# Windowed attention before two feed-forward layers on one core: fillers, weight words and first loads at the head

## Chip, cores, metric

One Trainium2 chip, one core of it. The metric is the device time of one execution in microseconds; the time of a kernel is the median over its runs. Before the change three runs gave 887.54 us in the median (884.97 to 889.1).

## What is computed

Two parts in a row, on 2304 tokens of 512 features. First attention: 4 batches, 8 heads of 64, 512 local and 32 global positions each; a local query sees the local keys within 32 positions and all global keys, a global query sees everything. Then two feed-forward layers, 512 to 2048 and back, with different functions in the middle.

```python
s_g = scale * q_g @ k_all.T                       # k_all: global, then local keys
out_g = softmax(s_g) @ v_all
s_ll = where(abs(i - j) <= 32, scale * q_l @ k_l.T, -1e9)
out_l = softmax(concat(scale * q_l @ k_g.T, s_ll)) @ concat(v_g, v_l)
x = concat(out_g, out_l)                          # tokens x 512
h = x @ moe_w_in;  x = (h * sigmoid(h)) @ moe_w_out
h = x @ moe2_w_in; y = (h * cos(h)) @ moe2_w_out
```

The weights are handed over as 64-bit floats; the kernel reads them as pairs of 32-bit words and makes 32-bit floats of them on the chip. Every product of the feed-forward layers is taken as three matmuls of a high and a low part.

## The kernel before

**Units.** The local attention is cut into units: one pair of heads, 256 queries, in four windows of 64. There are 32 units; the first eight, `EARLY`, are unit 0 to unit 7. They make up the inputs of the first feed-forward tile (512 tokens) and are done before it: this is the head. A unit has loads of k, of two halves of q (one a head, `load_qk`, lines 226 and 229) and of v (`load_v`, line 242), all issued from SP; its scores on TensorE (`unit_scores`, line 252); mask and maximum on VectorE (`unit_max`, line 268); the exponential on ScalarE (`unit_exp`, line 278); the normalisation on VectorE (`unit_norm`, lines 286 to 289); copies of the global columns on GpSimd (`unit_glob_parts`, lines 301 and 302); two groups of transposes on TensorE (lines 324 and 310) with their copies on ScalarE (lines 328 and 314); the products with the values on TensorE (`unit_values`, lines 351 and 358); and a high and a low part of the result, on ScalarE and VectorE (`unit_x`, lines 369 and 371).

**Fillers.** `keep_going` (line 337) issues matmuls of zeros into a part of a bank that nobody reads. `begin` does so between the first scores (8, 4, 6, 6 and 6 of 512 columns), and `unit_values` in every unit of the head, `PAUSE` = 6 of 256 columns before the products.

**Weights.** A chunk is one `(f, part)` of the first layer: 128 x 512 floats as pairs of words, 512 KB, loaded by `load_w1` (line 121). `rebias` shifts the high word (line 131) and the low word (line 132) on ScalarE; `to_f32` puts them together on VectorE (lines 138 and 142); `split_w_hi` makes the high part, on GpSimd for the chunks in `POOLED` (line 159) and on ScalarE for the others (line 161); `split_w_lo` the low part on VectorE (line 165). The first five chunks in the order of need are all in `POOLED`.

**Order.** All is planned by hand: `at(rank, step, fn, ...)` puts a function at a step, and `run` issues the steps in order and, within a step, by rank. `plan_early_unit` gives unit n its steps around n - 9: scores three steps earlier, maximum one step earlier, exponential, normalisation and copies at n - 9, transposes a step later, values two steps later. The shifts of chunk i fall on step i - 4, at a rank ahead of the GpSimd copies of a unit; its floats one step and its low part two steps later. Steps -12 to -1 are kept in this order as they stand; steps 0 to 35 may be reordered by the scheduler; from 36 on they are kept again. The first feed-forward tile begins at step 0. Each engine works through its queue in order, and so does SP. Ahead of all steps stand the loads: q and k of units 0, 1 and 2, v of unit 0, the global values, then unit 3, and so on, with the weight chunks from unit 5 on between them; a load waits until the eighth load before it has landed.

Of the kernel before, what the change touches and what calls it, by code (L numbers as in the profile page):

```python
# [11 lines left out]
F32 = mybir.dt.float32  # L12
# [3 lines left out]
AF = mybir.ActivationFunctionType  # L16
ALU = mybir.AluOpType
# [23 lines left out]
REBIAS = 2.0**-112  # L41
# [7 lines left out]
def attention_then_two_ffn(  # L49
# [9 lines left out]
    nc = tc.nc  # L59
# [56 lines left out]
    def slot(part, f, dtype=F32):  # L116
        return wts.tile([128, 1024], dtype, tag=f"w{part}_{f}", name="w")
# [10 lines left out]

    def rebias(ph, f, part):
        low, high = (W[ph, f, part][:, :, i] for i in range(2))  # L130
        nc.scalar.activation(out=high.bitcast(F32), in_=high.bitcast(F32), func=AF.Copy, scale=REBIAS)
        nc.scalar.activation(out=low, in_=low.bitcast(U32), func=AF.Copy, scale=TOP3, bias=TOP3_BIAS)

    def to_f32(ph, f, part):
# [81 lines left out]
    def load_qk(n):  # L216
        if n >= NU:
            return
        if n < EARLY:
            t = slot(1, NF - 1 - n)[:, 0 : UNIT * (64 + KX)]  # L220
        else:
            t = P["qk"].tile([128, UNIT * (64 + KX)], F32, tag="qk", name="qk")
        q = t[:, 0 : UNIT * 64].rearrange("p (c x) -> p c x", c=UNIT)
        k = t[:, UNIT * 64 :].rearrange("p (c x) -> p c x", c=UNIT)
        src = units[n, :, 0 : UNIT * 128].rearrange("p (c x) -> p c x", c=UNIT)
        nc.sync.dma_start(out=t[:, UNIT * 64 :], in_=units[n, :, UNIT * 128 : QKCOLS])
        for h in range(2):
            part = slice(64 * h, 64 * h + 64)
            nc.sync.dma_start(out=q[part], in_=src[part, :, part])
        A.setdefault(n, {}).update(q=q, k=k)  # L230

    def load_v(n):
# [101 lines left out]
    def keep_going(room, times):  # L334
        moving = zeros.unsqueeze(1).to_broadcast([128, room.shape[1] // 64, 64])
        for _ in range(times):
            nc.tensor.matmul(room[0:64], zeros, moving, start=True, stop=True, skip_group_check=True)
# [4 lines left out]
    def unit_values(n):  # L342
        b, p = n // (2 * NP), n % NP
        a = A[n]
        pool, tag = (ps_y, f"y{n % 2}") if n < EARLY else (ps_a, "a")
        bank = pool.tile([128, 512], F32, tag=tag, name="ps_o")
        a["po"] = po = bank[:, 0 : UNIT * 64].rearrange("p (c x) -> p c x", c=UNIT)
        if n < EARLY:
            keep_going(bank[:, UNIT * 64 :], PAUSE)
        for h in range(2):  # L350
            nc.tensor.matmul(
                po, vst[b][:, p, D * h : D * h + 128], a["pgt"][:, 2 * h : 2 * h + 2, :], start=h == 0, stop=False,
                skip_group_check=True,
            )
        for j in range(UNIT):
            for h in range(2):
                rows = slice(64 * h, 64 * h + 64)
                nc.tensor.matmul(  # L358
                    po[rows, j, :], a["v"][:, j, rows],
                    a["pt"][:, 2 * h + j // 2, 64 * (j % 2) : 64 * (j % 2) + 64], start=False, stop=j == UNIT - 1,  # L360
                    skip_group_check=True,
                )
# [410 lines left out]

    P, M, A, G, H, Y, gq, g32, vst, CH = ({} for _ in range(10))
    EARLY = 2 * NP
    PAUSE = 6
    LEAD, SLACK, LOADS, AHEAD, FIRST, CUT = 9, 3, 6, 8, -4, 36
    LAG = 12
    POOLED = (0, 1, 2, 3, 4, 6, 8, 10)
    head, pre, gemm, pe, post = -20, 0, 10, 20, 40  # L780
    seq = [(t, f) for t in range(len(size[0])) for f in range(NF)]
# [15 lines left out]
    def plan_early_unit(n, s):  # L797
        at(head + 9, s - 3, unit_scores, n)
        at(head, s - 1, unit_max, n)
        at(head + 1, s, unit_exp, n)  # L800
        at(head + 8, s, unit_norm, n)
        at(head + 8, s, unit_glob_parts, n)
        at(head + 4, s + 1, unit_local_t, n)
        at(head + 4, s + 1, unit_glob_parts_t, n)
        at(head + 5, s + 1, unit_p, n)
        at(head + 5, s + 1, unit_glob_parts_p, n)
        at(head + 2, s + 2, unit_values, n)
        at(head + 3, s + 2, unit_x, n, 0)
        at(head + 12, s + 2, unit_x, n, 1)
# [5 lines left out]
    def plan_unit(n, s, after):  # L815
        exp, norm, turn, parts, values, x = (s + i for i in after)
        at(pe + 1, s, unit_scores, n)
        at(post, s, unit_max, n)
        at(pre, exp, unit_exp, n)
        at(pre, norm, unit_norm, n)  # L820
        at(pe + 2, turn, unit_local_t, n)
        at(post, turn, unit_p, n)
        if after is NEAR:
            at(pre, norm, unit_glob_parts, n)
            at(gemm + 25, turn, unit_glob_parts_t, n)
            at(post, turn, unit_glob_parts_p, n)
        else:
            at(pre, turn, unit_glob_t, n)
            at(pre, parts, unit_glob_p, n)
        at(pe, values, unit_values, n)  # L830
        at(post, values, unit_x, n, 0)
        at(pre, x, unit_x, n, 1)
        at(post, s, load_qk, n + 2)
        at(post, values, load_v, n + 1)
# [33 lines left out]
    for b, s in ((1, 11), (2, 47), (3, 64)):  # L868
        plan_vg(b, s)

    chunks = sorted(
        (tick[i] if part == 0 else second[i], f, part)
        for i, (t, f) in enumerate(seq) if t == 0 for part in range(2)
    )
    for i, (need, f, part) in enumerate(chunks):
        s = min(need - SLACK, FIRST + i * (tick[NF] - 3 - FIRST) // (len(chunks) - 1))
        if i >= AHEAD:
            at(post, s - LOADS, load_w1, f, part)
        at(head + 6, s, rebias, 0, f, part)
        at(head + 7, s + 1, to_f32, 0, f, part)  # L880
        at(head + 10, s + 1, split_w_hi, 0, f, part)
        at(head + 6.5, s + 2, split_w_lo, 0, f, part)
# [8 lines left out]
    for i, (f, part) in enumerate(order):  # L891
        s = times[i]
        ready = max([times[i - 2] + 1 if i > 1 else 0, s - 2] + [e + 1 for e in ends if e < s])
        at(pre + 1, ready, load_w2_words, f, part)
        at(post - 1, s, rebias, 1, f, part)
        at(pre, s + 1, to_f32, 1, f, part)
        at(post - 1, s + 1, store_w2, f, part)
    for i in range(HALF):
        for row in (1, 0):
            f = i + HALF * row  # L900
# [51 lines left out]
    for q in range(pairs):  # L952
# [17 lines left out]
        for m, (row, c) in enumerate(todo):  # L970
            s_m = s + LAG + m * 7 // len(todo)
            if q == pairs - 2:
# [6 lines left out]
    attention_pools(p1)  # L979
    make_constants()  # L980
    load_qk(0)
    load_qk(1)
    load_qk(2)
    load_v(0)
# [101 lines left out]
```

## Time and profile before

| | |
|---|---|
| median of three runs | 887.54 us (884.97 to 889.1) |
| the profiled execution | 885.68 us |
| its span | 883.9 us |
| TensorE busy | 866.0 us, 98% |
| VectorE busy | 654.0 us, 74% |
| ScalarE busy | 515.8 us, 58% |
| GpSimd busy | 250.8 us, 28% |
| mean granted clock of TensorE | 0.996 |

The profile is of one execution; its span runs from the first to the last instruction of the program, and its own time is some 2 us longer. Engines are called PE (TensorE), PEld (TensorE's weight loads), DVE (VectorE), ACT (ScalarE), POOL (GpSimd) and SP; a q behind the name means the engine's sequencer. A line such as L131 is the line of the kernel. In a timeline, a row has start, duration, engine, line, operation, out<-in, the count of merged instructions, and in brackets the engine's idle time before it with what ended that. Small tiles share names: q, k, v of the first eight units and the weights are all `w`. The clock is given as a share of full speed.

### The profile page before, as it was taken

How to read it: one execution, taken by the hardware profiler on the slowest of the kernel's cores; microseconds unless marked ns; L12 is line 12 of the kernel's file. 1: busy time of each engine (PE TensorE's matmuls, PEld its weight loads, DVE VectorE, ACT ScalarE, POOL GpSimd, SP SyncE). 2: the span in 40 equal slices, each digit the busy share in tenths (PEclk: the TensorE clock that was granted, in tenths of full speed). 3: DMA queues.
4: the chain of work that ended last, by engine and by line, in shares of the span. 5: the costliest groups of instructions: out<-in, count | busy, mean ns of one | idle time of the engine just before them, and what ended most of it. 6: DMA issues, size and time to landing. Idle time of an engine off the chain costs nothing.

```text
span 883.9 us, 16714 instructions
## 1 busy us (share of the span) xinstructions
PE 866.0 (98%) x5854; PEld 759.2 (86%) x5854; DVE 654.0 (74%) x1531; ACT 515.8 (58%) x1171; POOL 250.8 (28%) x455
## 2 busy tenths in 40 slices
PE   8899999999999999999999999999999999999997
PEld 5677778899888999999988888888998889889996
DVE  4799993687979767677477667888887667876674
ACT  4898962566655655565355464565755446554453
POOL 3221110021222212011010044444444444455530
PEclk9999999999999999999999999999999999999999
DMA  8958520466555755444388769887567555576641
GB/s 264 352 177 290 201 66 13 156 205 195 173 169 160 224 170 159 134 130 145 125 289 277 256 184 295 247 225 188 116 168 196 118 119 119 122 202 143 143 108 60
DMA packets 126179, 156.57 MB, mean 177 GB/s; under 512 B 29072, under 2 KB 85904, under 8 KB 126096
## 3 DMA queue, kind: packets, MB, share of 16 engines
q1 hardware_dynamic: 77712, 111.44, 38.5%
q0 software_dynamic: 48384, 44.06, 21.8%
q8 instruction: 47, 0.77, 0.4%
q14 instruction: 36, 0.29, 0.1%
HBM read 123.47 MB, written 31.98 MB: 176 GB/s over the span
## 4 chain that ended last, share of the span: by engine, by line
PE 77%; DVE 7%; ACT 5%; DMA 3%; issue 2%; POOL 0%; SPq 0%; ACTq 0%; DVEq 0%
PE ps_y L760 7%; PE ps_y L761 7%; PE ps_y L759 7%; PE ps_p L688 6%; PE ps_p L689 6%; PE ps_p L690 6%; PE ps_y L524 6%; PE ps_hid L485 5%; PE ps_hid L487 5%; PE ps_hid L486 5%; PE ps_y L526 5%; PE ps_y L525 5%; PE ps_o L358 1%; PE ps_s L252 1%; DMA raw<-in_w_dram 1%
## 5 line engine op out<-in xcount | busy, mean ns | idle before, releaser
L627 POOL DMA_DIRECT2D w<-w1c x336 | 177.6, 535 | 255.4 <-PE ps_p L690 183.8
L524 PE MATMUL ps_y<-act,w 128*128 128x256 f32 (+2 forms) x384 | 131.8, 343 | 0.0
L485 PE MATMUL ps_hid<-xh,w 128*128 128x256 f32 (+2 forms) x384 | 126.5, 329 | 0.0
L526 PE MATMUL ps_y<-act,w 128*128 128x256 f32 (+2 forms) x384 | 126.1, 328 | 0.0
L525 PE MATMUL ps_y<-act,w 128*128 128x256 f32 (+2 forms) x384 | 126.0, 328 | 0.0
L486 PE MATMUL ps_hid<-xh,w 128*128 128x256 f32 (+2 forms) x384 | 125.8, 328 | 0.0
L487 PE MATMUL ps_hid<-xl,w 128*128 128x256 f32 (+2 forms) x384 | 125.7, 327 | 0.0
L760 PE MATMUL ps_y<-w,g 128*128 128x512 f32 x272 | 107.7, 396 | 0.0
L761 PE MATMUL ps_y<-w,g 128*128 128x512 f32 x272 | 107.4, 395 | 0.0
L759 PE MATMUL ps_y<-w,g 128*128 128x512 f32 x272 | 106.5, 392 | 0.6 <-DVE g L749 0.6
L688 PE MATMUL ps_p<-w 128*128 128x384 f32 (+1 forms) x320 | 105.1, 328 | 1.9 <-ACT area L701 1.8
L689 PE MATMUL ps_p<-w 128*128 128x384 f32 (+1 forms) x320 | 105.5, 330 | 0.0
L690 PE MATMUL ps_p<-w 128*128 128x384 f32 (+1 forms) x320 | 105.1, 329 | 0.0
L720 ACT ACTIVATE area<-area 128x768 int32<-128x768 f32 (+1 forms) x48 | 38.9, 811 | 103.0 <-DVE area L707 65.3
L497 DVE SCALAR_TENSOR_TENSOR act<-act,ps_hid 128x256 f32<-128x256 f32 (+2 forms) x96 | 50.6, 527 | 64.3 <-ACT act L496 64.1
L496 ACT ACTIVATE act<-ps_hid 128x256 f32<-128x256 f32 (+2 forms) x96 | 44.8, 467 | 88.8 <-PE ps_hid L487 88.7
L524 PEld LDWEIGHTS ps_y<-act,w 128*128 128x128 f32 x384 | 72.7, 189 | 10.8 <-issue 4.0
L485 PEld LDWEIGHTS ps_hid<-xh,w 128*128 128x128 f32 x384 | 73.0, 190 | 5.6 <-issue 0.4
L487 PEld LDWEIGHTS ps_hid<-xl,w 128*128 128x128 f32 x384 | 72.9, 190 | 5.2
L486 PEld LDWEIGHTS ps_hid<-xh,w 128*128 128x128 f32 x384 | 73.1, 190 | 4.9
L526 PEld LDWEIGHTS ps_y<-act,w 128*128 128x128 f32 x384 | 72.6, 189 | 5.1
L525 PEld LDWEIGHTS ps_y<-act,w 128*128 128x128 f32 x384 | 72.8, 189 | 4.5
(152 smaller groups left out, 1835.1 us busy)
## 6 DMA issues: line engine op xcount, KB each, us to landing
w<-w1c POOLq DMA_DIRECT2D x336, 128.0 KB, 2.4
w<-in_w_dram SPq DMA_DIRECT2D x32, 512.0 KB, 7.3
raw<-in_w_dram SPq DMA_DIRECT2D x64, 256.0 KB, 3.1
w1c<-w SPq DMA_DIRECT2D x44, 256.0 KB, 3.3
w2f<-w SPq DMA_DIRECT2D x64, 128.0 KB, 3.0
qk<-in_units_dram SPq DMA_DIRECT2D x24, 320.0 KB, 4.2
v<-in_units_dram SPq DMA_DIRECT2D x24, 256.0 KB, 3.2
w<-w2f SPq DMA_DIRECT2D x24, 256.0 KB, 5.1
```

The source lines that it names most:

```text
L485: nc.tensor.matmul(h, lo[:, ws], xh[:, k, :], start=k == 0, stop=False)
L486: nc.tensor.matmul(h, hi[:, ws], xh[:, k, :], start=False, stop=False)
L487: nc.tensor.matmul(h, hi[:, ws], xl[:, k, :], start=False, stop=k == NP - 1)
L524: nc.tensor.matmul(o, lo[:, ds_], gh, start=f == 0 and d % per == 0, stop=False, skip_group_check=True)
L525: nc.tensor.matmul(o, hi[:, ds_], gh, start=False, stop=False, skip_group_check=True)
L526: nc.tensor.matmul(o, hi[:, ds_], gl, start=False, stop=f == NF - 1, skip_group_check=True)
L627: nc.gpsimd.dma_start(out=part, in_=w1c[q % HALF][j][:, i * 256 : i * 256 + 256])
L688: nc.tensor.matmul(bank, lo, xh, start=whole and k == 0, stop=False, skip_group_check=True)
L689: nc.tensor.matmul(bank, hi, xh, start=False, stop=False, skip_group_check=True)
L759: nc.tensor.matmul(y, gl, hi, start=begin_, stop=False)
L760: nc.tensor.matmul(y, gh, hi, start=False, stop=False)
L761: nc.tensor.matmul(y, gh, lo, start=False, stop=end)
```

## The change

Three edits, all of them at the head. The fillers in the values of units 1 to 4 go, those of units 0, 5, 6 and 7 stay. The high words of the first five weight chunks are shifted by GpSimd instead of ScalarE; the low words stay with ScalarE. The q halves of units 0, 1 and 2 are issued from ScalarE's queue instead of SP's.

```diff
     def rebias(ph, f, part):
         low, high = (W[ph, f, part][:, :, i] for i in range(2))
-        nc.scalar.activation(out=high.bitcast(F32), in_=high.bitcast(F32), func=AF.Copy, scale=REBIAS)
+        if ph == 0 and (f, part) in [x[1:] for x in chunks[:BESIDE]]:
+            nc.gpsimd.tensor_scalar(
+                out=high.bitcast(F32), in0=high.bitcast(F32), scalar1=REBIAS, scalar2=1.0, op0=ALU.mult, op1=ALU.mult
+            )
+        else:
+            nc.scalar.activation(out=high.bitcast(F32), in_=high.bitcast(F32), func=AF.Copy, scale=REBIAS)
         nc.scalar.activation(out=low, in_=low.bitcast(U32), func=AF.Copy, scale=TOP3, bias=TOP3_BIAS)
...
         for h in range(2):
             part = slice(64 * h, 64 * h + 64)
-            nc.sync.dma_start(out=q[part], in_=src[part, :, part])
+            (nc.scalar if n < 3 else nc.sync).dma_start(out=q[part], in_=src[part, :, part])
...
-        if n < EARLY:
+        if n in LOOSE:
             keep_going(bank[:, UNIT * 64 :], PAUSE)
...
-    PAUSE = 6
+    PAUSE, LOOSE = 6, (0, 5, 6, 7)
...
-    LAG = 12
+    LAG, BESIDE = 12, 5
```

## Rows read from the trace of the kernel before

**Rows 1.** The page, section 1: busy time, share of the span, instructions:

```profile
PE 866.0 (98%) x5854; PEld 759.2 (86%) x5854; DVE 654.0 (74%) x1531; ACT 515.8 (58%) x1171; POOL 250.8 (28%) x455
```

**Rows 2.** The chain that ended last, in order of time: start, duration, what:

```profile
42.26 1.09 PE ps_tg L310 x4
...
55.43 0.69 DVE w L165
...
111.46 0.47 PE ps_o L351 x2
```

**Rows 3.** Windows: length, busy us of PE, PEld, DVE, ACT, POOL, clock, DMA, GB/s:

```profile
35.00:40.00 5.00, 3.00 (x33) 2.35 (x33) 3.47 (x11) 5.00 (x16) 1.56 (x4) 1.00 1.06 399
...
50.00:110.00 60.00, 58.69 (x378) 46.02 (x376) 57.94 (x129) 55.95 (x120) 9.50 (x15) 1.00 0.74 246
```

**Rows 4.** DMA view of 0:3 (40 slices, queue), 3:8, 8:13 with its q loads:

```profile
DMA  0000000000000000000000095868925529998999
...
q1 hardware_dynamic: 151, 0.31, 35.8%
...
q1 hardware_dynamic: 1709, 1.02, 73.5%
...
q1 hardware_dynamic: 1384, 1.42, 100.7%
...
w<-in_units_dram SPq DMA_DIRECT2D x4, 64.0 KB, 4.5
```

**Rows 5.** Timeline of SP, the q loads of units 0 and 3:

```profile
1.19 1.40 SPq L229 DMA_DIRECT2D w<-in_units_dram  x2
...
8.13 1.27 SPq L229 DMA_DIRECT2D w<-in_units_dram  x2
```

**Rows 6.** Timeline of ScalarE, its first exponential:

```profile
6.48 0.43 ACT L278 ACTIVATE w<-w,st 128x160 f32<-128x160 f32 x1 [4.46 <-DVE st L268]
```

**Rows 7.** Timeline of TensorE, the scores of units 3 and 7:

```profile
13.10 0.97 PE L252 MATMUL ps_s<-w 64*64 64x160 f32 x16 [1.39 <-DVE vst L193]
...
27.32 0.96 PE L252 MATMUL ps_s<-w 64*64 64x160 f32 x16 [0.18 <-DMA w<-in_units_dram]
```

**Rows 8.** Timeline of TensorE, fillers (L337) and values of units 3, 4, 7:

```profile
28.21 0.84 PE L337 MATMUL ps_o<-zeros 128*64 128x256 bf16 x6
...
28.98 0.50 PE L351 MATMUL ps_o<-pgt,vst 96*128 96x256 f32 x2
...
31.89 0.30 PEld L351 LDWEIGHTS ps_o<-pgt,vst 96*128 96x128 f32 x2 [0.27 <-ACT pgt L314]
...
43.28 1.49 PE L337 MATMUL ps_o<-zeros 128*64 128x256 bf16 x6
```

**Rows 9.** Timeline of ScalarE, the two shifts of chunk 0:

```profile
31.73 0.68 ACT L131 ACTIVATE w<-w 128x512 f32<-128x512 f32 x1
...
32.30 0.68 ACT L132 ACTIVATE w<-w 128x512 int32<-128x512 uint32 x1
```

**Rows 10.** Timeline of VectorE and GpSimd: copies, normalisations (L286), split of chunk 0:

```profile
31.07 0.56 POOL L301 TENSOR_SCALAR xl<-w 128x128 fp32r<-128x128 f32 x2 [2.56 <-DVE w L289]
...
34.66 0.17 DVE L286 TENSOR_SCALAR st<-st 128x4 f32<-128x4 f32 x1 [0.22 <-ACT w L278]
...
37.13 0.62 POOL L159 TENSOR_SCALAR w<-w 128x512 fp32r<-128x512 f32 x1
...
37.78 0.69 DVE L165 TENSOR_TENSOR w<-w 128x512 fp32r<-128x512 f32 x1 [1.43 <-POOL w L159]
...
39.72 0.16 DVE L286 TENSOR_SCALAR st<-st 128x4 f32<-128x4 f32 x1
```

**Rows 11.** Timeline of VectorE and GpSimd, decoding beside a GpSimd copy:

```profile
48.03 1.72 DVE L138 SCALAR_TENSOR_TENSOR w<-w 128x512 int32<-128x512 int32 x2
...
48.26 0.94 POOL L159 TENSOR_SCALAR w<-w 128x512 fp32r<-128x512 f32 x1 [2.65 <-ACT w L132]
```

**Rows 12.** Windows, columns as in rows 3: one microsecond:

```profile
43.00:44.00 1.00, 1.00 (x6) 0.61 (x5) 1.00 (x2) 0.56 (x2) 0.00 (x0) 0.50 0.30 75
```

## The prediction

> **What bounds the kernel now.** I read the page first: one core, TensorE busy for 98% of the span [rows 1]. So a change at the head counts only if the matmuls of the first feed-forward tile come earlier by it. The chain of waits tells what those wait for. It runs through TensorE at 42.26 us, then almost wholly over ScalarE and VectorE, which turn the 64-bit weight words into floats, and is back on TensorE for good at 111.46 us [rows 2]. Between 50 and 110 us VectorE is busy for 57.94 of 60 us [rows 3]: the decoding of weights is the bound there, and its order does not change. I therefore take whatever brings VectorE's decoding forward around 40 us as carried to the end, and nothing else.
>
> Then the head itself, from its start. The DMA queues are busy for 35.8% of the first 3 us, 73.5% of the next 5 and 100.7% of the 5 after that [rows 4]; the first bytes move in slice 24 of 40, at 1.7 us. Meanwhile SP issues one load after the other, the two q halves of a unit costing it 1.40 or 1.27 us [rows 5]. So SP's issue bounds the loads up to some 8 us, the DMA engines after that. TensorE feels it twice: the scores of unit 3 start after 1.39 us of waiting at 13.10 us, those of unit 7 after 0.18 us at 27.32 us [rows 7]. The first of these is put down to VectorE's split of the global values; I read it as unit 3's q halves, issued from 8.13 us for 1.27 us and landing 4.5 us after an issue, so at about 13 us [rows 4, 5], since no operand of the scores comes from that split.
>
> Later ScalarE fills up: from 35 to 40 us it is busy for all 5.00 us [rows 3]. The weight shifts, two of some 0.57 us a chunk from 31.73 us on, stand in its queue between two units' work [rows 9]. Behind it VectorE goes through one fixed loop a step: normalise unit 6 (34.66), GpSimd's copies of unit 6 and of chunk 0's high part (37.13), VectorE's low part of chunk 0 (37.78, after 1.43 us of waiting), chunk 1's words, normalise unit 7 (39.72) [rows 10].
>
> **The change, part by part.**
>
> *q halves from ScalarE's queue.* Six issues leave SP; six similar ones at 0.65 us (half of 1.27 to 1.40) [rows 5] make 3.9 us. ScalarE has them ahead of its first exponential, for which it now stands idle for 4.46 us until 6.48 us [rows 6]. The issues fit into that; queued behind them are that exponential and its table load, and behind these nothing that TensorE needs before the transposes of unit 0. I cost them at nothing; without that cover they would cost their 3.9 us. On SP every load from k of unit 1 on moves forward, the weight chunks and v included. But the landings move forward only by DMA time that was idle. From 1.7 to 8 us that is 6.3 − (0.358 × 3 + 0.735 × 5) = 6.3 − 4.75 = 1.55 us [rows 4]. The bounds are 0 and 3.9 us; I take 1.55, because the queues stand at 100.7% right after.
>
> The Trainium skill speaks against this part (DMA: Bandwidth & Descriptors, section "Issuing engines are not separate DMA queues"): issuing from several engines concurrently saves only the sequencer's issue time, since all run on the same DMA engines. By it alone this term would be nil and the sum that of rival A; the row for 3 to 8 us, with a quarter of the engines' time idle, says that here the issue time counts for a while.
>
> *Fillers.* Four groups of six matmuls go. One group holds TensorE from 28.21 to 28.98 us, 0.77 us, and the other three are alike [rows 8]. With the unit-3 wait gone and the fillers of units 1 and 2 out, TensorE would reach the scores of unit 7 by more than 1.55 us earlier (1.39 + 2 × 0.77 = 2.9), so it waits there for the DMA: the term of units 1 and 2 is covered by the landing, gain 0 beyond the 1.55. The filler of unit 3 stands directly behind those scores: gain 0.77. The filler of unit 4 ends in the shadow of ScalarE, since the values of unit 4 wait 0.27 us for its copy at 31.89 us [rows 8]: gain 0.
>
> *High words on GpSimd.* Chunk 0's shift leaves ScalarE's queue ahead of the exponentials of unit 6, 32.30 − 31.73 = 0.57 us [rows 9]; VectorE's normalisation of unit 6 waits for just these (0.22 us) [rows 10]: gain 0.57. Chunk 1's brings the exponentials of unit 7 forward, but their normalisation comes out of the loop of rows 10 and not from ScalarE: 0. Chunk 2's to 4's lie where ScalarE waits for others: 0. GpSimd pays five operations. The nearest row is its copy of 128 x 512 words, 0.94 us beside VectorE [rows 11]. They stand in its queue before the copies of the next unit, but before those it waits 2.56 us for VectorE [rows 10], in the other steps as long or longer; chunk 0's shift shows no wait for its DMA [rows 9], nor do the next four. So nothing is held up behind them. On VectorE the overlap costs: two word operations took 1.72 us beside that copy, against 2 × 0.69 for two of VectorE's decoding operations alone (the 0.69 of rows 10), 0.34 more [rows 11]. Bounds: 0 and 5 × 0.34 = 1.7. I take one, 0.34, for chunk 2, whose shift follows directly behind the copy that VectorE's loop waits for.
>
> **Sum.** −1.55 − 0.77 − 0.57 + 0.34 = −2.55 us. The profiled execution has 885.68 us, so 883.1; it lies 1.9 us under the median of the three runs, 887.54, and the median by the same sum is 885.0 us.
>
> **The rivals.**
>
> *A: the landings do not move.* The DMA engines, not SP, set the early pace, and q from a second queue only takes turns with k. For it: 73.5% is an average over small packets. Against it: SP is only at unit 3's q at 8.13 us [rows 5], when a quarter of the queues' time has gone unused. Then only −0.77 − 0.57 + 0.34 = −1.0 remains: 886.5.
>
> *B: SP's issue time comes back whole.* Landings move by up to 3.9 us, TensorE's own pace decides, 2.9 us at unit 7's scores: −2.9 − 0.77 − 0.57 + 0.34 = −3.9: 883.6. For it: the 1.39 us wait. Against it: 100.7% from 8 us on.
>
> *C: TensorE's clock falls without its fillers: slower than before.* The row for 43 to 44 us shows a granted clock of 0.50, the 1.2 GHz level, and a filler group there takes 1.49 us against 0.84 [rows 8, 12], after steps in which TensorE had waited on others. If the clock falls at the values of unit 2 and stays there through those of unit 6, five steps, each has at least 2.1 us of needed work (28.98 to 31.89 less a filler) [rows 8], 1.77 times as long: 5 × 1.6 = 8.1, less 2.55, or +5.5: 893.0. It decides from two such steps on (3.2 against 2.55). Against it: without fillers the unfilled steps are shorter, and the waits in them stay under 1 us. The Trainium skill (TensorE: Matmul & The Clock Gate, section "What's actually happening") says the same in general: the default state is throttled and activity releases it, a rule against taking fillers out.
>
> *D: the clock holds at the end of the head.* ScalarE is relieved and the waits before 42 us shrink. Then the filler's 0.65 and, by the same factor, 0.47 of the four transposes at 42.26 us [rows 2, 8] come back too: −3.7: 883.8. Against it: VectorE, not TensorE, bounds what follows.
>
> *E: nothing arrives.* The steps around 45 to 110 us are ordered automatically, and another order eats the gain: 887.5.
>
> **How the numbers follow.** Chances: forecast 0.42, A 0.14, B 0.16, C 0.10, D 0.10, E 0.08. A measurement of this kernel tells about 0.5%, 4.4 us, from no change: faster means under 883.1. That takes B with half its weight (0.08, B and D together give 882.4), D half (0.05) and a quarter of the forecast, where the medians scatter by 2 us (0.11): 0.24. Slower, over 892.0, is C: 0.10. The rest, 0.66, is within. The range goes from 881.5 (B and D with a little scatter) to 888.8 (E with scatter) and leaves C out.
>
> **What would show it.** Right: SP's loads from v of unit 0 on come earlier, ScalarE has six issues before its table load; no wait of over 1 us before unit 3's scores; unit 7's scores still wait for DMA, near 25.8 us; the normalisation of unit 6 near 32.1 us and of unit 7 near 37.2; five GpSimd operations of 0.6 to 1 us; the chain back on TensorE for good near 109 us. Wrong: unit 7's scores without wait and near 24.4 us (B) or still at 27.3 us (A); a granted clock of 0.50 before 31 us (C); the gain there at 45 us but not at 111 us (E).

## The result and the profile after

The change made the kernel slower: 891.11 us in the median against 886.88 us for the kernel before, 22 runs each, ratio 1.0054 [1.0040, 1.0068]. That is 4.23 us more by the medians and 4.8 us by the ratio. The profiled execution took 893.51 us, its span is 891.7 us. From line 131 on, the lines of the kernel before stand five lower in the changed one; L132 is there GpSimd's shift.

The page, section 1, after: TensorE's share fell by a point [rows 1], since it waited more.

```profile
PE 868.6 (97%) x5830; PEld 761.9 (85%) x5830; DVE 656.2 (74%) x1531; ACT 513.5 (58%) x1166; POOL 258.4 (29%) x460
```

The chain that ended last, after. The columns are start, duration, what.

```profile
66.33 6.57 DMA w<-in_w_dram
...
89.99 6.64 DMA w<-in_w_dram
...
114.06 0.63 ACT act L501
...
116.03 0.47 PE ps_o L356 x2
```

TensorE takes the chain over for good at 116.03 us, 4.57 us later than at 111.46 us [rows 2]. Before that the chain stands twice on a load of weights, 6.57 and 6.64 us. The chain before has one such piece too, 6.12 us from 63.62 us, a row that I had not read. From 96.65 to 114.69 us the chain then runs over ScalarE; that of before runs over VectorE from the piece below, at 98.11 us, to 111.31 us.

```profile
98.11 0.69 DVE act L505
```

The two traced executions lie 7.83 us apart (893.51 and 885.68 us), so 4.57 us of this come ahead of 116 us and 3.3 us behind it. Here are the windows from 200 to 300 us, before and after, columns as in rows 3.

```profile
200.00:300.00 100.00, 95.94 (x1034) 87.60 (x1034) 81.77 (x292) 61.57 (x206) 20.68 (x26) 1.00 0.60 184
200.00:300.00 100.00, 96.00 (x1004) 89.10 (x1005) 81.53 (x287) 62.06 (x203) 22.50 (x28) 0.95 0.60 180
```

The change's trace has the clock at 1.2 GHz (0.50) in three stretches of 3.41 us here, from 206.94, 258.14 and 295.69 us; before has none. Around them the change falls from 4.96 us behind (an activation at 194.82 us, before at 189.86) to 7.25 us behind (at 312.97 us, before at 305.72).

Windows, after, columns as in rows 3.

```profile
35.00:40.00 5.00, 3.95 (x43) 2.73 (x42) 3.51 (x10) 4.92 (x16) 2.19 (x6) 1.00 1.05 390
43.00:50.00 7.00, 6.09 (x33) 4.50 (x34) 5.63 (x10) 3.55 (x8) 3.15 (x6) 0.51 0.30 105
50.00:110.00 60.00, 57.11 (x357) 44.25 (x356) 54.48 (x123) 51.34 (x112) 11.65 (x16) 1.00 0.74 243
```

ScalarE still works 4.92 of the 5 us from 35 to 40. The granted clock was at its lower level, 1.2 GHz (0.51), from 43.10 to 49.93 us; before, it was so from 42.09 to 45.50 us. VectorE is busy for 54.48 us from 50 to 110 us instead of 57.94 [rows 3]: it waits there.

The DMA view, after: the two queues' packets, megabytes and share in 3:8 and 8:13, and last the q loads of ScalarE's queue in 0:13, with the median time to landing.

```profile
q1 hardware_dynamic: 573, 1.20, 76.4%
q10 hardware_dynamic: 1117, 0.27, 25.4%
...
q1 hardware_dynamic: 772, 0.59, 49.4%
q10 hardware_dynamic: 491, 0.12, 12.4%
```

```profile
w<-in_units_dram ACTq DMA_DIRECT2D x6, 64.0 KB, 5.9
```

The engines are full from 3 to 8 us now (76.4 + 25.4%, 73.5% before), and stand at 49.4 + 12.4% from 8 to 13 us, where they were full before [rows 4]. So the early gap was closed and a larger one opened. Why, the timelines of SP and of ScalarE tell, and SP's waits in 0:13 (us in all, times, longest).

```profile
0.74 1.48 SPq L231 DMA_DIRECT2D w<-in_units_dram  x3
2.26 0.61 SPq L247 DMA_DIRECT2D w<-in_units_dram  x1
...
4.83 0.35 SPq L231 DMA_DIRECT2D w<-in_units_dram  x1
9.38 1.39 SPq L234 DMA_DIRECT2D w<-in_units_dram  x2
```

```profile
0.73 7.25 ACTq L234 DMA_DIRECT2D w<-in_units_dram  x6
8.01 1.28 ACT L283 ACT_TABLE_LOAD   x1 [8.01 <-DMA w<-in_units_dram]
9.31 0.43 ACT L283 ACTIVATE w<-w,st 128x160 f32<-128x160 f32 x1
```

```profile
SPq L234 <- DMA w<-in_units_dram: 4.2, 1, 4.2
```

SP issues k of units 0, 1 and 2 and v of unit 0 within 2.1 us, 1.2 MB, beside the q halves of 64 KB in small packets that unit 0 needs. The six issues on ScalarE take 7.25 us, not the 3.9 us of my reckoning: in the trace the loads of both queues take eight completion semaphores in turn, and an issue waits until the load that had its semaphore before has landed (the sixth is issued at 7.38 us, when the second has landed at 7.36 us). By the same rule SP stands 4.2 us in front of unit 3's q, until unit 1's half from ScalarE's queue has landed at 9.4 us. The first exponential comes at 9.31 us [rows 6: 6.48].

TensorE, timeline after: scores (L257) of units 0, 1, 3 and 7, the last filler.

```profile
7.40 0.77 PE L257 MATMUL ps_s<-w 64*64 64x160 f32 x14 [2.12 <-DMA w<-in_units_dram]
...
9.50 0.88 PE L257 MATMUL ps_s<-w 64*64 64x160 f32 x16 [0.35 <-DMA w<-in_units_dram]
...
13.84 0.78 PE L257 MATMUL ps_s<-w 64*64 64x160 f32 x16
...
28.52 0.97 PE L257 MATMUL ps_s<-w 64*64 64x160 f32 x16
...
44.92 1.49 PE L342 MATMUL ps_o<-zeros 128*64 128x256 bf16 x6
```

Unit 0 waits 2.12 us for its second q half. By unit 3 the head is 0.74 us late, by unit 7 1.20 us [rows 7]. GpSimd and VectorE, timelines after: shifts (L132), words (L143, L147), low parts (L170), normalisations (L291).

```profile
28.93 0.66 POOL L132 TENSOR_SCALAR w<-w 128x512 f32<-128x512 f32 x1
...
33.28 1.73 POOL L132 TENSOR_SCALAR w<-w 128x512 f32<-128x512 f32 x2
```

```profile
33.39 1.10 DVE L143 SCALAR_TENSOR_TENSOR w<-w 128x512 int32<-128x512 int32 x1
34.52 1.02 DVE L147 SCALAR_TENSOR_TENSOR w<-w 128x512 int32<-128x512 int32 x1
35.47 0.16 DVE L291 TENSOR_SCALAR st<-st 128x4 f32<-128x4 f32 x1
...
38.57 1.12 DVE L170 TENSOR_TENSOR w<-w 128x512 fp32r<-128x512 f32 x1 [1.42 <-POOL w L164]
...
40.94 0.16 DVE L291 TENSOR_SCALAR st<-st 128x4 f32<-128x4 f32 x1
...
44.47 1.12 DVE L170 TENSOR_TENSOR w<-w 128x512 fp32r<-128x512 f32 x1 [1.20 <-POOL w L164]
```

### The profile page after: what moved, and what is told of

Same layout as the page of the kernel before. It is cut to its first block, busy times and chain, and to the rows that moved or that the text cites. A ratio compares the mean times of both kernels' runs of the same rounds, so it can differ in the third digit from the quotient of the medians.

```text
span 891.7 us, 16660 instructions
## 1 busy us (share of the span) xinstructions
PE 868.6 (97%) x5830; PEld 761.9 (85%) x5830; DVE 656.2 (74%) x1531; ACT 513.5 (58%) x1166; POOL 258.4 (29%) x460
## 4 chain that ended last, share of the span: by engine, by line
PE 84%; ACT 5%; DVE 5%; DMA 4%; issue 1%; SPq 0%; POOL 0%; ACTq 0%; DVEq 0%; POOLq 0%
PE ps_y L765 7%; PE ps_y L766 7%; PE ps_y L764 7%; PE ps_y L529 6%; PE ps_p L693 6%; PE ps_hid L492 6%; PE ps_hid L490 6%; PE ps_p L694 6%; PE ps_p L695 6%; PE ps_hid L491 6%; PE ps_y L530 6%; PE ps_y L531 6%; PE ps_s L257 2%; PE ps_o L363 2%; DMA w<-in_w_dram 1%; PE ps_t L329 1%
## 5 line engine op out<-in xcount | busy, mean ns | idle before, releaser
L529 PEld LDWEIGHTS ps_y<-act,w 128*128 128x128 f32 x384 | 73.6, 192 | 10.7 <-issue 3.8
L490 PEld LDWEIGHTS ps_hid<-xh,w 128*128 128x128 f32 x384 | 74.0, 193 | 5.3 <-ACT w L137 0.4
L491 PEld LDWEIGHTS ps_hid<-xh,w 128*128 128x128 f32 x384 | 73.9, 192 | 5.0
L531 PEld LDWEIGHTS ps_y<-act,w 128*128 128x128 f32 x384 | 73.6, 192 | 5.2
L530 PEld LDWEIGHTS ps_y<-act,w 128*128 128x128 f32 x384 | 73.7, 192 | 4.6
```

Of the source, the lines that this page charges most:

```text
L490: nc.tensor.matmul(h, lo[:, ws], xh[:, k, :], start=k == 0, stop=False)
L491: nc.tensor.matmul(h, hi[:, ws], xh[:, k, :], start=False, stop=False)
L529: nc.tensor.matmul(o, lo[:, ds_], gh, start=f == 0 and d % per == 0, stop=False, skip_group_check=True)
L530: nc.tensor.matmul(o, hi[:, ds_], gh, start=False, stop=False, skip_group_check=True)
L531: nc.tensor.matmul(o, hi[:, ds_], gl, start=False, stop=f == NF - 1, skip_group_check=True)
```

## The experiments

The first four take the change apart. Against the kernel before, the edits are these, the first in **queue_only**, the second in **fill_only**, the third (with the branch in `rebias`) in **pool_only**, the last two in **no_queue**.

```diff
-            nc.sync.dma_start(out=q[part], in_=src[part, :, part])
+            (nc.scalar if n < 3 else nc.sync).dma_start(out=q[part], in_=src[part, :, part])
...
-    PAUSE, LOOSE = 6, (0, 1, 2, 3, 4, 5, 6, 7)
+    PAUSE, LOOSE = 6, (0, 5, 6, 7)
...
-    LAG, BESIDE = 12, 0
+    LAG, BESIDE = 12, 5
```

> The q halves of units 0 to 2 from ScalarE's queue alone; fillers and shifts as before. Theory L (loads: q lands late beside SP's larger loads, and SP then waits for it; in the trace after the change unit 0's second half lets its scores start at 7.40 us instead of 5.18) expects the same start, scores of unit 7 over 1 us later than 27.32 us, and +1.5 to +4 us in time. Theory G (GpSimd beside VectorE) and theory F (clock without fillers) expect at most +1 us here.

> The high words of five chunks on GpSimd alone. Theory G (VectorE's decoding operations grow from 0.69 to 1.0 to 1.1 us beside GpSimd's shift, in the loop that normalises units 6 and 7) expects +1.5 to +3 us. Theories L and F expect -1 to +0.5 us (the 0.57 us of ScalarE gained, one overlap of 0.34 us lost).

> The fillers of units 1 to 4 left out alone. Theory F (the clock is at 1.2 GHz for longer before the first tile, 6.5 us instead of 3.3 after the change) expects +1.5 to +4 us and a granted clock of 0.50 over more than 4 us before 55 us. Theories L and G expect -1.5 to 0 us and a clock as before the change.

> The change without its queue part: q from SP, fillers out, shifts on GpSimd. Theory L expects no loss: -2 to +0.5 us against before. Theories G and F expect most of the +4.8 us of the whole change to stay: +2.5 to +5.

All the runs are in one table: the ratio to the kernel before with its interval, the mean granted clock of a run (median over the runs), and three times of the one traced execution: from when the clock was recorded as full, the start of unit 7's scores, and from when the chain stays with TensorE.

| kernel | ratio | mean clock | full from, us | scores 7, us | TensorE for good, us |
|---|---|---|---|---|---|
| before | | 0.996 to 0.997 | 4.54 | 27.32 | 111.46 |
| the change | 1.0054 [1.0040, 1.0068] | 0.992 | 5.55 | 28.52 | 116.03 |
| queue_only | 1.0036 [1.0017, 1.0055] | 0.9935 | 13.49 | 30.17 | 115.89 |
| pool_only | 1.0055 [1.0039, 1.0071] | 0.994 | 5.70 | 27.91 | 116.29 |
| fill_only | 1.0014 [0.9999, 1.0030] | 0.9955 | 3.95 | 27.67 | 115.50 |
| no_queue | 1.0031 [1.0012, 1.0049] | 0.992 | 5.38 | 27.51 | 112.38 |
| after_kept | 1.0040 [1.0023, 1.0057] | 0.992 | 13.22 | 28.70 | 113.83 |
| queue_only_kept | 1.0012 [0.9997, 1.0028] | 0.996 | 13.68 | 30.17 | 113.65 |
| pool_only_kept | 1.0004 [0.9989, 1.0020] | 0.9945 | 6.29 | 27.56 | 112.47 |
| fill_only_kept | 1.0006 [0.9988, 1.0024] | 0.996 | 6.08 | 27.28 | 112.03 |
| order_only | 1.0015 [0.9994, 1.0036] | 0.9945 | 9.96 | 28.80 | 112.68 |
| no_queue_kept | 0.9993 [0.9971, 1.0014] | 0.994 | 4.78 | 26.73 | 110.98 |
| queue_unit0_kept | 0.9994 [0.9975, 1.0014] | 0.9945 | 3.89 | 25.61 | 109.53 |
| fill_loads | 0.9985 [0.9964, 1.0005] | 0.9955 | 3.61 | 26.71 | 110.37 |
| after_unit0_kept | 1.0011 [0.9987, 1.0034] | 0.9925 | 5.32 | 25.56 | 110.37 |
| no_fill_kept | 1.0042 [1.0025, 1.0060] | 0.9915 | 5.55 | 28.85 | 114.02 |
| unit0_loads | 0.9994 [0.9981, 1.0007] | 0.997 | 9.10 | 27.18 | 111.15 |
| unit0_fill_loads | 0.9974 [0.9954, 0.9995] | 0.996 | 10.13 | 27.04 | 111.88 |

Each of the three suspicions finds its sign in its own kernel: unit 7's scores come 2.85 us later in **queue_only** (some 1.3 us of it with the clock, full only from 13.49 us: **no_fill_kept** below has the same loads, a full clock from 5.55 us and 28.85 us), VectorE's words of chunk 0 take 1.11 and 1.02 us and the normalisation of unit 7 comes at 40.53 us in **pool_only**, and the clock is low for 6.83 us from 41.49 us in **fill_only**. But none of these accounts for what was measured. **queue_only**, 3.2 us, lies in the range of theory L, but **no_queue** keeps 2.7 us of loss where L expected none; **pool_only** costs more than theory G had and **fill_only** less than theory F. No part helps, and the parts do not add: by the ratios they cost 3.2 (queue), 4.9 (pool) and 1.2 us (fill), which make 9.3, and the whole change 4.8. **pool_only** has its head 0.59 us late at unit 7's scores and is 4.83 us late at 116 us. The three parts have one thing in common: in steps 0 to 35 the order of the instructions is not that of before in any of them.

**With the order kept.** So the same kernels were run with the order of before in these steps. `ORDER` holds the positions, engine by engine; the edges ask for the order of issue and for no wait.

```diff
+        for one, two in zip(row, row[1:]):
+            tc.add_manual_dep(two, one.name, edge, reason="order of before")
...
+    begin_at = len(nc.cur_bb.bb.instructions)
     run(0, CUT)
+    keep_order(tc, nc.cur_bb.bb.instructions[begin_at:])
```

> The whole change, with the order of every engine's instructions in steps 0 to 35 tied to the order that the kernel before has there (edges of issue order alone, no waits); only what the change itself moves stands elsewhere. Theory O (order): most of the loss of the change comes from the automatic scheduler's other order in steps 0 to 35, since the three parts alone cost 3.2, 4.9 and 1.2 us and together 4.8, and since most of the difference arises between 49 and 110 us. With the order kept the time is then 886 to 888.5 us beside 886.9 (ratio 0.999 to 1.002), and the ninth activation of the first product (103.2 us before, 107.7 after) is back within 1.5 us of before. Theory D (direct): the late q loads, the overlap on VectorE and the clock cost it themselves; the order of the kernel before, made for earlier inputs, only waits longer: ratio 1.005 or more, the ninth activation at 107 us or later.

> The q halves of units 0 to 2 from ScalarE's queue alone, order of steps 0 to 35 kept as before. Theory O: the head is as late as with the automatic order (scores of unit 7 at about 30.2 us beside 27.3), but much of it is taken up by 110 us: ratio 1.000 to 1.002. Theory D: the delay of the loads of 2.8 us is carried to the end: ratio 1.003 to 1.004, as measured without the kept order (1.0036).

> The five high shifts on GpSimd alone, order of steps 0 to 35 kept as before. Theory O: the overlap with VectorE costs 0.8 us at the probabilities of unit 7 and 1.2 us at its transposes, and that is all: ratio 1.000 to 1.002. Theory D: 1.004 to 1.006, as measured without the kept order (1.0055).

> The fillers of units 1 to 4 left out alone, order of steps 0 to 35 kept as before. Theory O: the 0.4 us that the head gains stay, less what the half clock from 41.5 to 48.3 us takes (about 1 us at the first activation): ratio 0.999 to 1.001. Theory D: 1.001 to 1.002 as without the kept order (1.0014), the half clock being its whole price.

With its own order GpSimd's part costs 0.55%, with the order of before 0.04%, and the two intervals do not touch: all but a fraction of what the shifts cost came from the order. The chain of **pool_only_kept** has one weight load where that of **pool_only** has two, and TensorE has it 3.8 us earlier.

```profile
70.01 5.22 DMA w<-in_w_dram
...
87.48 6.96 DMA w<-in_w_dram
...
116.29 0.47 PE ps_o L356 x2
```

```profile
69.40 6.90 DMA w<-in_w_dram
...
112.47 0.47 PE ps_o L356 x2
```

With the order kept each single part has no change within its interval. For the whole change theory O fell: 1.0040 lies outside its 0.999 to 1.002, and the ninth activation, at 105.02 us, between the two theories. **fill_only_kept** shows something else. Its first activation comes at 47.05 us, 2.1 us earlier than before, and TensorE has the chain 0.6 us later than before. Between lies this piece of its chain, and SP's timeline; the single row below is the kernel before's.

```profile
68.75 9.36 DMA w<-in_w_dram
```

```profile
66.95 0.80 SPq L389 DMA_DIRECT2D gv<-in_glob_dram  x2
67.80 4.65 SPq L121 DMA_DIRECT2D w<-in_w_dram  x7
```

```profile
68.99 5.12 SPq L121 DMA_DIRECT2D w<-in_w_dram  x7
```

Seven weight loads stand behind the two loads of global values (L389), which wait for a buffer, and then land in one burst of 9.36 us. I took this for what ate the lead, and the next runs test it. The trace says otherwise: the kernel before has the same seven loads in the same place, and the lead is 1.20 us ahead of the burst (an activation at 65.94 us, before at 67.14) and still 1.03 us behind it (82.19 us, before at 83.22). It is lost just after, where the clock stands at 1.2 GHz from 84.59 to 88.00 us; before has it at full there. Here are the window from 84 to 88 us and two matmuls of the chain, at the lower clock and at the full one.

```profile
84.00:88.00 4.00, 4.00 (x12) 3.10 (x12) 3.87 (x12) 4.00 (x8) 0.64 (x2) 0.57 0.71 219
```

```profile
85.15 0.43 PE ps_hid L490
...
88.14 0.23 PE ps_hid L491
```

The activation that follows comes at 89.38 us, 0.46 us later than before's 88.92.

**Order alone, q alone, the burst.** Four more: **order_only** gives the kernel before the order of the changed one, **no_queue_kept** is fillers and shifts with the order kept, **queue_unit0_kept** and **fill_loads** are **queue_only_kept** and **fill_only_kept** with these edits, the second an excerpt of SP's row of `ORDER`, in which 21 weight loads move ahead:

```diff
-            (nc.scalar if n < 3 else nc.sync).dma_start(out=q[part], in_=src[part, :, part])
+            (nc.scalar if n < 1 else nc.sync).dma_start(out=q[part], in_=src[part, :, part])
...
-57-59 85 115 139 183 181-182 234 260 232-233 290 329 379
+59 85 115 139 183 57-58 234 260 181-182 290 329 379
```

> Nothing of the change but the order: the work of the kernel before (fillers, shifts on ScalarE, q from SP), with the engines' order in steps 0 to 35 tied to the one that the scheduler chose for the changed kernel. Theory O: tying the changed kernel to the order of before saved 0.14% (1.0054 to 1.0040), of GpSimd's part alone 0.5%, so the other order by itself costs 1.5 to 3 us: ratio 1.0015 to 1.0035, and the 64th step of the second product, at 158.7 us before, comes at 161 us or later. Rival M (mismatch): an order costs only where it does not fit the inputs it was made for; then this one, made for late loads and put on early ones, is worth nothing by itself or costs far more than 3 us (1.005).

> Fillers of units 1 to 4 out and the five shifts on GpSimd, q from SP as before, order of steps 0 to 35 kept. If the parts add once the order is kept (1.0006 and 1.0004, each within its interval of no change), the ratio is 0.999 to 1.002, and of the 1.0040 of the whole change with the order kept the q loads are the larger part. If the fillers and the shifts act on each other (the half clock falling onto the late transposes), it is 1.003 or more, as without the kept order (1.0031).

> Only the two q halves of unit 0 from ScalarE's queue, those of units 1 and 2 from SP; order kept. Theory S (shared completions and many small packets at once): unit 0's second half still lands later than the 5.14 us of before, since the larger loads that SP now issues earlier run beside it, but SP no longer stands behind a late q half, so unit 1's scores start within 0.7 us of the 6.86 us of before and those of unit 7 at 27.0 to 28.2 us; ratio 0.999 to 1.001. Theory Q (ScalarE's queue itself lands late): unit 0's second half at about 7.4 us as in the change, scores of unit 1 after 9 us, unit 7 after 29 us; ratio 1.001 or more.

> Fillers of units 1 to 4 out, order kept, but in SP's order of steps 0 to 35 the weight loads stand ahead of the loads of global keys, values and queries that wait for buffers (21 loads moved, nothing else). Theory B (burst): with the order kept the head without fillers was 2.1 us ahead at the first activation (47.05 against 49.19 us) and 0.6 us behind at the 64th step of the second product (159.29 against 158.68), because seven weight loads stand behind such a load until 67.8 us and land in one burst 9.4 us long. With the loads ahead the gain is kept: 64th step at 155.5 to 157.5 us, ratio 0.996 to 0.999. Rival V: VectorE, which works 59 of the 61 us from 49 to 110, sets the pace there, and the waits for weights lie beside it: 64th step at 158 us or later, ratio 0.999 to 1.002.

**order_only** came to 1.0015, at the lower edge of what theory O had, its 64th step at 160.25 us a little under it, and its interval holds no change as well as the whole expected cost. **no_queue_kept** is the clearest: with q back on SP the ratio goes from 1.0040 to 0.9993, and the intervals do not touch. With the order kept, the q loads are what costs. **queue_unit0_kept** bears out theory S. Here are TensorE's scores of units 0, 1 and 7, and SP's first issues in it.

```profile
5.78 0.77 PE L257 MATMUL ps_s<-w 64*64 64x160 f32 x14 [1.07 <-DMA w<-in_units_dram]
...
7.45 0.77 PE L257 MATMUL ps_s<-w 64*64 64x160 f32 x16
...
25.61 0.91 PE L257 MATMUL ps_s<-w 64*64 64x160 f32 x16
```

```profile
0.74 0.86 SPq L231 DMA_DIRECT2D w<-in_units_dram  x2
1.66 1.41 SPq L234 DMA_DIRECT2D w<-in_units_dram  x2
...
5.05 0.61 SPq L247 DMA_DIRECT2D w<-in_units_dram  x1
```

The same queue, used for two halves instead of six, gives unit 1's scores 2.05 us earlier than in the change and those of unit 7 1.71 us earlier than before; SP is never held for a completion as long as a microsecond. Theory S expected 27.0 to 28.2 us for unit 7; 25.61 us is better than that. So it is not ScalarE's queue that is late. In **fill_loads** no weight load is left on the chain before 84 us and the 64th step comes at 157.61 us, as theory B had it but for 0.11 us; the median is 1.2 us under before's, but the interval reaches to 1.0005. It does not bear theory B out, though: its clock is full from 44.57 us to 110 us, so it also lacks the stretch from 84.59 us in which **fill_only_kept** lost its lead, and the two causes are not told apart.

**What was left.** Four last runs: **after_unit0_kept** is **after_kept** with `n < 1`, **no_fill_kept** is **after_kept** with all the fillers, **unit0_loads** and **unit0_fill_loads** join unit 0's q on ScalarE's queue to the weight loads moved ahead, with the fillers of units 1 to 4 and without.

> The whole change, order of steps 0 to 35 kept, but only unit 0's q halves from ScalarE's queue. Theory L (the late q of units 1 and 2 is what is left): scores of unit 7 at 25.5 to 26.5 us (28.7 with all three units moved, 27.3 before), ratio 0.996 to 1.000 where the whole change with the order kept had 1.0040. Theory X (the parts lose together for another reason, the clock above all): 1.002 or more though the head is earlier.

> The q halves of units 0 to 2 from ScalarE's queue and the five shifts on GpSimd, all fillers as before, order kept. Theory C (late q and missing fillers lose together: the clock rose only at 13.2 us and was back at half in four stretches, 14.5 us in all): with the fillers fewer such stretches, ratio 1.001 to 1.002, the sum of the two parts alone (1.0012 and 1.0004). Theory L: the fillers do not matter, the late units do: 1.003 to 1.004 as with the whole change.

> Unit 0's q halves from ScalarE's queue, and in SP's order of steps 0 to 35 the weight loads ahead of the global loads; fillers and shifts as before, order otherwise kept. Theory B (the loads stood in the way): of the 3.1 us that unit 0's q alone won at the first activation (46.11 beside 49.19 us) and of which 1.9 were left at the 64th step (156.81 beside 158.68), more stays: 64th step at 155 to 156.3 us, ratio 0.996 to 0.998. Rival V (VectorE sets the pace from 49 to 110 us): 64th step at 156.5 us or later, ratio 0.9985 to 1.000.

> The same without the fillers of units 1 to 4. Theory B: 64th step at 154 to 155.5 us, ratio 0.994 to 0.997. Rival V: no more than unit 0's q or the loads alone, ratio 0.998 to 1.000. If the clock falls for 6.83 us at about 40 us as in the changed kernel, the fillers' part is lost again: ratio as with the fillers or 0.1% above.

**no_fill_kept**, 1.0042, rules theory C out: putting the fillers back changes nothing. The clock stays low with them too (0.9915 in the median, and in the trace at 1.2 GHz for 6.83 us from 43.09 us), so this rules out the fillers, not the clock. **after_unit0_kept**, 1.0011 with unit 7's scores at 25.56 us, lies between what the two theories had; with 0.9993 for all q on SP it says that the late q of units 1 and 2 is the larger part of the 0.40%, though the intervals of **after_kept** and **after_unit0_kept** overlap. **unit0_loads** sits inside its rival's range, and its 64th step came at 158.35 us, past theory B's 156.3: no more of the gain stayed. **unit0_fill_loads** is the one version that is faster than the kernel before, and so than both: 0.9974 [0.9954, 0.9995], 884.56 us against 885.3 us. That lies between theory B and its rival. Among 17 versions, one interval that leaves out no change so narrowly may be chance. The execution that was traced, with its 64th step at 159.09 us and the clock low for 6.83 us from 40.85 us, was the slowest of its runs, 887.62 us.

**The clock, run by run.** One thing goes with the time in every kernel and was in no run's edit: the mean granted clock. Over the 34 or 35 runs of before in each of the four rounds, a straight line through time and clock gives 0.5 to 0.8 us more for each 0.001 less. The change has 0.992 where before has 0.996 to 0.997. By that line the difference would go with some 2 to 4 us, an estimate, of the 4.2 us: a large part of the loss goes with a clock at 1.2 GHz, in the change's trace also at 200 to 300 us, far behind the head. What makes the clock fall there is not shown; no run changed the clock and nothing else.

## Why the prediction was wrong

The forecast was 885.0 us, in a range of 881.5 to 888.8 us, and no change clear of noise; measured were 891.11 us, 4.23 us more than before.

**The step that failed is the first term, −1.55 us for landings that move forward.** Its sign was wrong, and so was its lower bound of 0. I had priced the six issues by SP's duration and asked only what stood behind them on ScalarE. The forecast that SP's loads come earlier was right (v of unit 0 at 2.26 us), and that was the harm: the large loads of k and v that nobody needed yet took DMA time from unit 0's q, and the shared completions then held both queues. Unit 7's scores started at 28.52 us, not near 25.8, the normalisations of units 6 and 7 at 35.47 and 40.94 us, not near 32.1 and 37.2, and the chain is TensorE's from 116.03 us, not from 109. At the end this costs, with the order kept, the difference of **after_kept** and **no_queue_kept**, 0.47% or 4.2 us; with the change's own order it is that of the change and **no_queue**, 0.23% or 2.0 us, and there the intervals overlap. The term of the kind that I had in mind exists, with two issues moved instead of six: −1.71 us at unit 7's scores in **queue_unit0_kept**, and −1.62 us between **unit0_loads** and **order_only**, which both have a full clock only from 9 to 10 us. The time does not show it: 0.9994 in **queue_unit0_kept** and in **unit0_loads**.

The Trainium skill (DMA: Bandwidth & Descriptors, section "Issuing engines are not separate DMA queues") has loads of all engines interleave on the same DMA engines. The rows after agree, with 76.4 and 25.4% from 3 to 8 us; by that rule the term would have been nil, and the loss from interleaving with the wrong loads is not in it.

**"Carried to the end" failed too.** I took VectorE's decoding as the only bound of 50 to 110 us and its order as unchanged. The clock is a second one: in **fill_only_kept**, 1.5 of the 2.1 us gained at the first activation were lost around the stretch from 84.59 to 88.00 us at 1.2 GHz. That weight loads are a third is not shown: they stand on the chain, but also on that of before. And the order did change, and the chain of the change stands on ScalarE from 96.65 to 114.69 us; rival E, which said that another order may come, had it only take the gain away. In the parts alone it cost 2.2 to 3.8 us at the point where TensorE takes over (queue_only, fill_only, pool_only against the kept ones). In the whole change that is 116.03 against 113.83 us, while the ratios, 1.0054 and 1.0040, have intervals that overlap.

**The fillers**, −0.77 us, were right in size: the normalisation of unit 7 came at 38.91 us in **fill_only_kept** against 39.72, 0.81 us earlier; of the time nothing of it shows (1.0006 [0.9988, 1.0024]). **The shifts** were not: −0.57 + 0.34 was to gain 0.23 us, and in **pool_only_kept** the same normalisation came at 40.18 us, 0.46 us later. The term that was mis-sized is the overlap. Four operations of VectorE grew from 0.69 to 1.10, 1.02, 1.12 and 1.12 us (33.39 to 44.47 us above), 1.6 us in all and near the bound of 1.7, where I took one at 0.34. Three of them, 1.2 us, stand ahead of unit 7's normalisation, and in **pool_only_kept** they took 1.09, 1.03 and 1.12 us.

**Rivals A, B and D** had the head no later than before, and it was later. **Rival C** had a slower kernel by a lower clock, but put it at the values of units 2 to 6 and down to the fillers. In the trace the clock fell at 43.10 us, for 6.83 us where before has 3.41 us, and the fillers made no difference in **no_fill_kept**. From the last filler to the first activation the change went from 1.64 us behind (44.92 and 43.28 us) to 3.51 us behind (52.70 and 49.19 us), 1.1 us of it by the matmul at 49.77 us (before at 47.06), in this longer stretch.

Open stays why q and shifts together cost 0.42% (**no_fill_kept**) when they cost 0.12 and 0.04% apart. TensorE had the chain there only 0.37 us later than in **queue_only_kept**, and the traced execution, 886.6 us, is 2.2 us under its kernel's median, so that trace cannot show the rest. The clock goes with it: 0.9915 in the median, against 0.996 and 0.9945 for the two apart.

## What to carry to other kernels

A second issuing queue lets every load start earlier, the ones not yet needed too: move as few as remove the wait, and look at what the first queue will send in their place and which completions the two share. Where part of a kernel is ordered automatically, run each edit with the old order tied as well, or the measurement is of two changes. And a gain counts only past every stage that it goes through: read what the chain stands on there, and the granted clock of each stretch, not only which engine is busy. Before a wait is given as the reason for a lost lead, see how large the lead was ahead of it and behind it.

## What the runs showed of the hardware

The first rise of TensorE's clock is not fixed. The head of **order_only** is that of the kernel before, instruction for instruction, but its last 14 scores of unit 0 took 1.33 us instead of 0.77 and unit 7's came at 28.80 us instead of 27.32. First the row of before, then those of **order_only**:

```profile
5.18 0.77 PE L252 MATMUL ps_s<-w 64*64 64x160 f32 x14 [0.20 <-DMA w<-in_units_dram]
```

```profile
5.54 1.33 PE L257 MATMUL ps_s<-w 64*64 64x160 f32 x14 [0.25 <-DMA w<-in_units_dram]
...
11.34 0.78 PE L257 MATMUL ps_s<-w 64*64 64x160 f32 x16
...
28.80 0.77 PE L257 MATMUL ps_s<-w 64*64 64x160 f32 x16
```

The 0.78 us for the 16 scores of unit 2 are at full speed; the clock was recorded as full from 9.96 us on there, from 4.54 us in the trace of before, and from 3.6 to 13.7 us over all the runs, at the latest three times in kernels with six q issues on ScalarE. A head read from a single trace is uncertain by over a microsecond for this alone, and so are the two right columns of the table; kernels with a like "full from" compare best.

Two operations of GpSimd and two of VectorE ran from 33.28 to 35.54 us, 2.26 us, where one after the other they would take 2 × 0.66 + 2 × 0.69 = 2.70. The Trainium skill (SBUF — State Buffer, section "Who interferes with whom") says that a VectorE instruction with two inputs in SBUF contends with a GpSimd instruction that reads SBUF, and calls contention for the port pair that the two engines share an exclusive lock. The rows agree that both take longer (1.73 us for GpSimd's two, 1.10 and 1.02 us for VectorE's), and show somewhat less than a full exclusion.
